# Linear attention feeding two layers on one core: reciprocals on 96x6 through a DMA reshape, the product a step later, and 3.5 slots to a pair of heads

## The chip, the cores and the metric

The kernel runs on one core of a Trainium2 chip. The metric is the device time of one execution in microseconds (us); the kernel before takes 976.46 us, the median of 3 runs (976.12 to 977.76). Engines are named as in the profile: PE (TensorE's matmuls), PEld (its weight loads), DVE (VectorE), ACT (ScalarE), POOL (GpSimd) and SP (SyncE, whose queue issues the DMAs).

## The reference

Three stages in a row, 64-bit weights in, float32 out:

```python
def phi(x):                                   # q, k: (4, 8, 576, 64), w_phi: (64, 128)
    proj = x @ w_phi
    proj = proj - max(abs(proj), axis=-1)
    return concatenate([exp(proj), exp(-proj)])
q_p, k_p = phi(q), phi(k)
kv  = einsum('bhsf,bhsd->bhfd', k_p, v);  z = sum(k_p, axis=2)
num = q_p @ kv;  den = q_p @ z + 1e-06
x = (num / den) as 2304 tokens x 512          # attention's output
x = leaky(x @ w_in) @ w_out                   # first layer, max(0.01 h, h), d_ff 2048
x = silu(x @ w_in2) @ w_out2                  # second layer, h / (1 + exp(-h))
```

## The kernel before

Heads are taken two at a time: 16 pairs. Pairs 0 to 7 are computed in float32 in a prologue (`num_full`). Pairs 8 to 15 are split into a high and a low part (`krh`, `krl`, `qs`, `qh`, `ql`, `KVH`, `KVL`), each product being the sum of three cheaper matmuls, and are computed in the gaps of the first layer (`num_split`, two parts of 288 tokens each).

The first layer has 5 tiles of tokens (`tiles1`) and 16 chunks of 128 hidden features. One chunk of one tile is a slot: there are 80. In a slot `emit_h` runs 12 matmuls (line 528); ACT makes `g` (line 531) and its high part `gh` (401), DVE the rest `gl = g - gh` (`sub`, line 122, the helper behind every `...l` or `...s` tile); `emit_y` of the slot before then runs 12 matmuls on `gh` and `gl` (line 547). In the first 16 slots the weights are also loaded as raw 64-bit numbers, narrowed by DVE (lines 394 to 397: `t`, `r`) and split; later ones come back from DRAM (`load_wo`, line 485, three buffers).

The steps of attention are called at times of a table: `OFF0` for the pairs of the prologue, `OFF1` for the split ones, plus a start `ts` for each pair. Before each half of a slot, `run_att(T0 + STEP * ...)` runs all steps whose time has come; `STEP = W / 4` makes a pair last 4 slots. `missing(t)` makes sure that a tile's tokens are all there before its first slot. A step of pair i, in the order of a pair: `lv`, `lq` load, `sp` splits, `pq0`, `pq1` project q (PE, then an all-reduce of the absolute maximum on POOL, line 223), `pk0`, `pk1`, `pkt` project k (DVE `km` line 152, `ke` line 153, ACT exp), `eq0`, `eq1` make `m`, `qh`, `ql`, `kv` the sums, `num0`, `num1` the quotient. After these calls a scheduler orders the instructions of each engine, so that the order on an engine isn't that of the calls.

In `num_split` the matmuls of line 329 leave in one PSUM bank 64 rows of numerator and 64 rows that all hold the same denominator: ACT copies those to `d` (line 332), DVE takes the reciprocal of 128x288 (line 333) and multiplies each half out of PSUM (line 336), and `put_x` splits the result into the first layer's `xh` and `xl`.

When attention is over, each slot gives 2.0 of credit to `run_jobs`, which prepares the second layer's weights (`prep_wi2`, `prep_wo`, `prep_wo2`, each job at a cost of 1.5 to 3.0). The second layer follows: u = 0 plain, u = 1 and 2 by a scheme of seven products (lines 597, 689, 769).

Of the kernel before, what the change touches and what calls it, by code (L numbers as in the profile page):

```python
# [8 lines left out]
F32 = mybir.dt.float32  # L9
F32R = mybir.dt.float32r  # L10
U32 = mybir.dt.uint32
AF = mybir.ActivationFunctionType
# [7 lines left out]
def tile_linear_attention_ffn_ffn(ctx: ExitStack, tc: tile.TileContext, q, k, v, w_phi, w_in1, w_out1, w_in2, w_out2, out):  # L20


    nc = tc.nc
    B, H, S, D = 4, 8, 576, 64
# [5 lines left out]
    HP = H // 2  # L30
# [3 lines left out]
    RAWB = 2  # L34
    NFULL = 8
    ABUFS0 = dict(kr=3, kt=3, qr=3, va=3, ke=2, p=2, m=2, qh=2, x=2)
    ABUFS1 = dict(kr=2, kt=2, qr=2, va=2, qh=2, ql=2)
    NKV, NNUM = 112, 96
    MIN64, MAX64 = 2.0**-15, 122872.0

# [5 lines left out]
    drp = ctx.enter_context(tc.tile_pool(name="drp", bufs=1, space=DRAM))  # L46
# [5 lines left out]
    def at(shape, dt, tag):  # L52
        return att_pool[0].tile(shape, dt, tag=tag, bufs=AB[0].get(tag, 1), name=tag)
# [28 lines left out]
        nc.vector.tensor_sub(BDL, BDF, BDH.bitcast(F32))  # L82


    tiles1 = [(0, 464)] + [(464 + 460 * i, 460) for i in range(4)]
    X1 = {}

    def x1_tile(t):
# [12 lines left out]
                yield t, lo - a, lo - t0, hi - lo  # L101

    P = [dict() for _ in range(B * HP)]

    def load_qk(i):

        st = P[i]
        st["kr"] = at([128, S0], F32, "kr")
# [15 lines left out]
    def full(i):  # L124
        return i < NFULL
# [102 lines left out]
    def s_eq(a):  # L228
        def f(i):
            st = P[i]  # L230
            c0, n = part(i, a)
            p, m = st["p", a], st["m", a]
            nc.vector.tensor_sub(m, p, m)
            qh = at([128, 2, 2 * n], F32 if full(i) else F32R, "qh")
            st["qh", a] = qh
            if full(i):
                nc.scalar.activation(qh[:, 0], m, AF.Exp)
                nc.scalar.activation(qh[:, 1], m, AF.Exp, scale=-1.0)
                return
# [36 lines left out]
    def put_x(i, rows, src, t0, n):  # L276

        b, hp = i // HP, i % HP
        for t, o, s0, n in segments(b * S + t0, n):
            xh, xl = x1_tile(t)  # L280
            nc.scalar.activation(xh[rows, hp, o : o + n], src[:, s0 : s0 + n], AF.Copy)
            sub(xl[rows, hp, o : o + n], src[:, s0 : s0 + n], xh[rows, hp, o : o + n])
# [34 lines left out]
    def num_split(i, a):  # L317
        st = P[i]
        c0, w = part(i, a)
        d = at([128, w], F32, "d")  # L320
        r = at([128, w], F32, "r")
        x = at([128, w], F32, "x")
        pn = [aps("num"), aps("num")]
        for j in range(2):
            o = pn[j][:, 0:w]
            todo = [(s, g, m) for s in range(2) for g, m in (("KVH", "qh"), ("KVH", "ql"), ("KVL", "qh"))]
            for n, (s, g, m) in enumerate(todo):
                lhs = st[g][:, j, s].rearrange("p t d -> p (t d)")
                nc.tensor.matmul(o, lhs, st[m, a][:, s, j * w : (j + 1) * w], start=(n == 0), stop=(n == 5))  # L329
            den = slice(64, 128) if j == 0 else slice(0, 64)  # L330
            num = slice(0, 64) if j == 0 else slice(64, 128)
            nc.scalar.activation(d[num], o[den], AF.Copy, bias=1e-6)
        nc.vector.reciprocal(r, d)
        for j in range(2):
            num = slice(0, 64) if j == 0 else slice(64, 128)
            nc.vector.tensor_mul(x[num], pn[j][num, 0:w], r[num])
        put_x(i, slice(0, 128), x, c0, w)

    def s_num(a):
        return lambda i: (num_full if full(i) else num_split)(i, a)  # L340

    W, WP = 8.0, 5.0
    fns = dict(
        lq=load_qk, lv=load_v, sp=s_split, pq0=s_pq(0), pq1=s_pq(1),
        pk0=s_pk(0), pk1=s_pk(1), pkt=s_pkt, eq0=s_eq(0), eq1=s_eq(1), kv=s_kv, num0=s_num(0), num1=s_num(1),
    )
    OFF0 = dict(lq=1.1, lv=3.08, sp=3.09, pq0=4.48, pk0=5.33, pk1=5.331, pq1=6.8, eq0=9, pkt=9.13, kv=9.131, num0=11.3, eq1=12.07, num1=16)
    OFF1 = dict(lv=-2.1251, lq=-2.1250, sp=0.5, pq0=2.1172, pk0=4.0606, pk1=4.0616, pq1=4.7479, eq0=6.2094, pkt=7.3391, kv=8.3898, num0=12.1423, eq1=13.9119, num1=14.457)
    END0 = max(OFF0.values()) + 1
    END1 = max(OFF1.values()) + 1  # L350
    ts = [WP * i for i in range(NFULL)]
# [4 lines left out]
    def missing(t):  # L356
        a0, n0 = tiles1[t]
        for _, i, n_ in seq:
            if n_ in ("num0", "num1"):
                c0, w = part(i, int(n_[3]))  # L360
                lo = i // HP * S + c0
                if lo < a0 + n0 and lo + w > a0:
                    return True
        return False

    def run_att(until, tile_=None):
        while seq and (seq[-1][0] < until or (tile_ is not None and missing(tile_))):
            if seq[-1][1] == NFULL and AB[0] is ABUFS0:
                att0_ctx.close()
                att_pool[0] = att_ctx.enter_context(tc.tile_pool(name="att1", bufs=1))  # L370
                AB[0] = ABUFS1
            _, i, n_ = seq.pop()
# [417 lines left out]
    RATE = (9.0, 9.0)  # L790
    s1p = [None]
    PRE = 4
    STEP = W / 4
    T0 = ts[HP - 1] + END0 - 1.15
    make_consts()
    for c in range(PRE):
# [5 lines left out]

    def jobs_of(p):
        for _ in prep_wi2(p):
            yield p, 1.8
        yield p, 1.6
        for f in range(2):
            prep_wo(1, 2 * p + f)
            yield p, 3.0

    def later_jobs():
        for p in range(NC // 2):
            for _ in prep_wo2(p):
                yield NP + p, 1.6
            yield NP + p, 1.5

    jobs = (x for f in (lambda: (x for p in range(NP) for x in jobs_of(p)), later_jobs) for x in f())
    credit, at_p = [0.0], [0]

    def run_jobs(more, upto=-1):  # L820
        credit[0] += more
# [5 lines left out]
    for s, (t, c) in enumerate((t, c) for t in range(len(tiles1)) for c in range(NC)):  # L827
        if t == 0 and c + PRE < NC:
            prep_wi(0, c + PRE)
        wo[c] = prep_wo(0, c) if t == 0 else load_wo(0, c)  # L830
        run_att(T0 + STEP * (s + 0.5) + 0.21, t if c == 0 else None)
        emit_h(t, c)
        run_att(T0 + STEP * (s + 1) + 0.21)
        if prev is not None:
            emit_y(*prev)
        prev = (t, c)
        if not seq and s1p[0] is None:
            att_ctx.close()
# [126 lines left out]
```

## Time and profile before

| | us |
|---|---|
| median of 3 runs | 976.46 (976.12 to 977.76) |
| the profiled execution | 977.25 |
| its span | 975.5 |
| PE busy | 953.0 (98%) |
| DVE busy | 662.0 (68%) |
| ACT busy | 577.1 (59%) |
| POOL busy | 72.6 (7%) |

The span runs from the first to the last instruction; the 1.75 us left of the execution lie around it. An engine is busy while an instruction other than register, branch, semaphore and DMA-issuing ones runs on it. The granted clock is TensorE's, as a share of 2.4 GHz.

### The profile page before, as it was taken

The page shows a single profiled execution, that of the slowest core. Times are in us where ns is not written, and L with a number is a line of the kernel's source. Part 1 is how long each engine was busy: PE and PEld are TensorE (multiplying, and loading weights), DVE is VectorE, ACT ScalarE, POOL GpSimd, SP SyncE. Part 2 cuts the span into 40 slices and gives each one's busy share as a digit, 9 for nine tenths or more (in the row PEclk, how much of TensorE's full clock was granted, in tenths as well). Part 3 has the DMA queues.
Part 4 walks back from the last instruction along what each step waited for, and adds up shares of the span by engine and source line. Part 5 has one row for each costly group of instructions (what it writes and reads, how often), then busy time and mean ns, then how long its engine had stood idle before and what let it go on. Part 6 is the DMA issues. An engine that isn't in the chain of part 4 may idle for free.

```text
span 975.5 us, 15291 instructions
## 1 busy us (share of the span) xinstructions
PE 953.0 (98%) x5328; PEld 879.7 (90%) x5328; DVE 662.0 (68%) x1236; ACT 577.1 (59%) x1171; POOL 72.6 (7%) x38
## 2 busy tenths in 40 slices
PE   7889999989999999999999999999999999999998
PEld 6778888879999999999899999988889999999998
DVE  7998448998666787557667765764557778625853
ACT  6776556676566666555546555664555666544553
POOL 3323200011111111100000000000000000000000
PEclk9999999999999999999999999999999999999999
DMA  8562036874332521218997999998899988897884
GB/s 277 163 207 89 2 131 215 312 240 153 102 96 91 165 86 59 87 52 305 370 322 258 385 412 361 348 374 269 301 357 321 396 271 288 292 296 221 248 275 147
DMA packets 100557, 227.86 MB, mean 234 GB/s; under 512 B 10368, under 2 KB 29568, under 8 KB 100480
## 3 DMA queue, kind: packets, MB, share of 16 engines
q1 hardware_dynamic: 100192, 226.62, 67.3%
q8 instruction: 43, 0.70, 0.3%
q14 instruction: 34, 0.28, 0.1%
q10 hardware_dynamic: 288, 0.26, 0.1%
HBM read 173.36 MB, written 53.48 MB: 233 GB/s over the span
## 4 chain that ended last, share of the span: by engine, by line
PE 83%; DVE 9%; DMA 5%; ACT 2%; issue 1%; SPq 0%; DVEq 0%; ACTq 0%
PE ps_a L528 17%; PE ps_y L547 17%; PE ps_y L769 12%; PE ps_a L597 6%; PE ps_a L689 6%; PE ps_y L689 5%; PE ps_y L630 5%; PE ps_a L262 3%; PE ps_a L329 3%; PE ps_a L630 2%; DMA raw<-in_moe_w_in_dram 2%; DMA raw<-in_moe_w_out_dram 2%; DVE t L396 2%; PE ps_a L296 1%; PE ps_y L262 1%
## 5 line engine op out<-in xcount | busy, mean ns | idle before, releaser
L547 PE MATMUL ps_y<-gh,wo 128*128 128x460 f32 (+1 forms) x640 | 197.0, 372 | 1.6 <-ACT gh L401 1.6
L547 PEld LDWEIGHTS ps_y<-gh,wo 128*128 128x128 f32 x640 | 119.5, 188 | 14.6 <-ACT gh L401 2.4
L547 PE MATMUL ps_y<-gl,wo 128*128 128x460 f32 (+1 forms) x320 | 119.0, 372 | 2.5 <-DVE gl L122 2.4
L528 PE MATMUL ps_a<-xh,wih 128*128 128x460 f32 (+1 forms) x320 | 120.1, 375 | 0.0
L528 PE MATMUL ps_a<-xh,wil 128*128 128x460 f32 (+1 forms) x320 | 118.8, 371 | 0.0
L528 PE MATMUL ps_a<-xl,wih 128*128 128x460 f32 (+1 forms) x320 | 118.7, 371 | 0.0
L769 PE MATMUL ps_y<-gt,ws 128*128 128x384 f32 x672 | 118.2, 337 | 0.0
L769 PEld LDWEIGHTS ps_y<-gt,ws 128*128 128x128 f32 x672 | 117.7, 188 | 0.0
L223 POOL PARTITION_ALL_REDUCE m<-p x32 | 72.0, 2252 | 340.3 <-ACT p L219 199.2
L122 DVE TENSOR_TENSOR gl<-g,gh 128x460 fp32r<-128x460 f32 (+1 forms) x80 | 55.3, 691 | 39.7 <-ACT gh L401 39.0
L531 ACT ACTIVATE g<-ps_a 128x460 f32<-128x460 f32 (+1 forms) x80 | 44.2, 552 | 58.2 <-PE ps_a L528 55.5
L689 PE MATMUL ps_a<-xs,ws 128*128 128x384 f32 x378 | 71.8, 336 | 0.6 <-DVE g L668 0.5
L547 PEld LDWEIGHTS ps_y<-gl,wo 128*128 128x128 f32 x320 | 60.1, 188 | 9.6 <-DVE gl L122 3.4
L689 PEld LDWEIGHTS ps_a<-xs,ws 128*128 128x128 f32 x378 | 66.0, 188 | 1.6 <-DVE g L668 0.8
L528 PEld LDWEIGHTS ps_a<-xh,wil 128*128 128x128 f32 x320 | 60.2, 188 | 6.7
L528 PEld LDWEIGHTS ps_a<-xh,wih 128*128 128x128 f32 x320 | 60.2, 188 | 6.3 <-issue 0.3
L597 PE MATMUL ps_a<-xs,ws 128*128 128x384 f32 x336 | 65.7, 338 | 0.0
L528 PEld LDWEIGHTS ps_a<-xl,wih 128*128 128x128 f32 x320 | 60.2, 188 | 6.1
L597 PEld LDWEIGHTS ps_a<-xs,ws 128*128 128x128 f32 x336 | 60.0, 188 | 3.1 <-DVE hs L589 0.3
L392 ACT ACTIVATE t<-raw 128x512 f32<-128x512 f32 x64 | 42.7, 668 | 32.1 <-DMA raw<-in_moe_w_out_dram 16.2
L401 ACT ACTIVATE gt<-g 128x384 fp32r<-128x384 f32 x80 | 41.8, 524 | 33.6 <-PE ps_y L769 33.1
L122 DVE TENSOR_TENSOR gt<-g,gt 128x384 fp32r<-128x384 f32 x80 | 44.2, 555 | 23.8 <-ACT gt L401 23.5
(168 smaller groups left out, 1852.7 us busy)
## 6 DMA issues: line engine op xcount, KB each, us to landing
ws<-wis SPq DMA_DIRECT2D x168, 256.0 KB, 5.2
wo<-wos SPq DMA_DIRECT2D x80, 512.0 KB, 5.1
raw<-in_moe_w_in_dram SPq DMA_DIRECT2D x32, 512.0 KB, 5.0
raw<-in_moe_w_out_dram SPq DMA_DIRECT2D x32, 512.0 KB, 5.4
wos<-wo SPq DMA_DIRECT2D x32, 512.0 KB, 5.1
ws<-wo SPq DMA_DIRECT2D x64, 256.0 KB, 4.1
wis<-wst SPq DMA_DIRECT2D x24, 512.0 KB, 6.4
ws<-wos SPq DMA_DIRECT2D x48, 256.0 KB, 3.9
```

The source lines that it names most:

```text
L122: nc.vector.tensor_tensor(out_, x, h.bitcast(F32), op=ALU.subtract)
L223: nc.gpsimd.partition_all_reduce(m, p, 128, bass_isa.ReduceOp.absmax)
L262: nc.tensor.matmul(pv[:, s, j], ke[:, 2 * c + j, s, :], vf[:, w : w + NKV], start=False, stop=(j == 1 and c == 3), skip_group_check=True)
L392: nc.scalar.activation(t, hi.bitcast(F32), AF.Abs)
L401: nc.scalar.activation(h, f, AF.Copy)
L528: nc.tensor.matmul(ph, a[:, kk, :], b_[:, kk, :], start=(m == 0), stop=(m == 3 * KD - 1))
L531: nc.scalar.activation(g, ph, AF.Prelu, alpha=0.01)
L547: nc.tensor.matmul(Y[t][d][:, 0:n], a[:, ds_], b_, start=(c == 0 and m == 0), stop=(c == NC - 1 and m == 2))
L597: nc.tensor.matmul(bank[b_], w[:, a, kk], x[:, c, kk], start=(first and m == 0), stop=(m == 5), skip_group_check=True)
L630: nc.tensor.matmul(Y[u][r], a[:, rs], hl[f][:, b_], start=(p == 0 and f == 0 and m == 0), stop=(p == NC // 2 - 1 and f == 1 and m == 2))
L689: nc.tensor.matmul(bank[b_], w[:, a, kk], x[:, c, kk], start=(first and m == 0), stop=(m == 5), skip_group_check=True)
L769: nc.tensor.matmul(bank[b_][db], w[:, a, db], t[:, c], start=(first and p == 0 and m == 0), stop=(p == NP - 1 and m == 2), skip_group_chec ...
```

## The change

Six edits, made together.

- In `num_split` ACT copies one row of denominators (1x288) for each half and the numerators (64x288) to `x`. The two rows go by DMA into `e6` (96x6), DVE takes the reciprocal there, a DMA writes it to `rec` in DRAM, and two DMAs broadcast it back over 64 partitions each into `d`.
- The product of `x` and `d` and `put_x` move to new steps `fin0`, `fin1`, at 16 and 18.3 in `OFF1`; `missing` looks for these.
- `x` and `d` get two buffers each.
- `pkt` moves from 7.3391 to 5.1 in `OFF1`.
- `STEP` is `W / 3.5`, so a pair lasts 3.5 slots; `tiles1` is 462, 462, 460, 460, 460 in place of 464 and four of 460.
- `settle` ends a half-done job of weight preparation before the next part of the second layer's `x` is prepared.

```diff
-    ABUFS1 = dict(kr=2, kt=2, qr=2, va=2, qh=2, ql=2)
+    ABUFS1 = dict(kr=2, kt=2, qr=2, va=2, qh=2, ql=2, x=2, d=2)
...
-    tiles1 = [(0, 464)] + [(464 + 460 * i, 460) for i in range(4)]
+    tiles1 = [(462 * i, 462) for i in range(2)] + [(924 + 460 * i, 460) for i in range(3)]
...
+    rec = drp.tile([B * HP, 2, S], F32, name="rec")
...
         d = at([128, w], F32, "d")
-        r = at([128, w], F32, "r")
-        x = at([128, w], F32, "x")
+        x = st["x", a] = at([128, w], F32, "x")
...
-            den = slice(64, 128) if j == 0 else slice(0, 64)
+            den = slice(64, 65) if j == 0 else slice(0, 1)
             num = slice(0, 64) if j == 0 else slice(64, 128)
-            nc.scalar.activation(d[num], o[den], AF.Copy, bias=1e-6)
-        nc.vector.reciprocal(r, d)
+            nc.scalar.activation(d[den], o[den], AF.Copy, bias=1e-6)
+            nc.scalar.activation(x[num], o[num], AF.Copy)
+
+        e = at([96, w // 48], F32, "e6")
         for j in range(2):
-            num = slice(0, 64) if j == 0 else slice(64, 128)
-            nc.vector.tensor_mul(x[num], pn[j][num, 0:w], r[num])
-        put_x(i, slice(0, 128), x, c0, w)
+            nc.sync.dma_start(e[48 * j : 48 * j + 48], d[64 - 64 * j : 65 - 64 * j])
+        nc.vector.reciprocal(e, e)
+        nc.sync.dma_start(rec[i, a].rearrange("(p f) -> p f", p=96), e)
+        st["r", a] = d
+        for j in range(2):
+            nc.sync.dma_start(d[64 * j : 64 * j + 64], rec[i, a, j * w : (j + 1) * w].unsqueeze(0).to_broadcast([64, w]))
+
+    def s_fin(a):
+        def f(i):
...
+            nc.vector.tensor_mul(x, x, st["r", a])
+            put_x(i, slice(0, 128), x, c0, w)
...
-    OFF1 = dict(lv=-2.1251, lq=-2.1250, sp=0.5, pq0=2.1172, pk0=4.0606, pk1=4.0616, pq1=4.7479, eq0=6.2094, pkt=7.3391, kv=8.3898, num0=12.1423, eq1=13.9119, num1=14.457)
+    FIN = 16
...
+    OFF1 = dict(lv=-2.1251, lq=-2.1250, sp=0.5, pq0=2.1172, pk0=4.0606, pk1=4.0616, pq1=4.7479, eq0=6.2094, pkt=5.1, kv=8.3898, num0=12.1423, eq1=13.9119, num1=14.457, fin0=FIN, fin1=FIN + 2.3)
...
-            if n_ in ("num0", "num1"):
+            if n_ in ("fin0", "fin1"):
...
-    STEP = W / 4
+    STEP = W / 3.5
...
+    def settle():
+
+        while half[0]:
+            credit[0] -= next(jobs)[1]
```

Since the steps fall into other slots, the scheduler gives each engine another order. Three places show it.

The first is DVE's order from the `gl` of slot 10 to that of slot 12, in the stretch where the last weights are narrowed (`t`, `r`, `wo`). Before:

```order
L122 TENSOR_TENSOR gl<-g,gh 128x464
L122 TENSOR_TENSOR qs<-qr,qs 64x576 x2
L122 TENSOR_TENSOR wo_1808<-r_1810,wo_1808 128x512
L122 TENSOR_TENSOR gl<-g,gh 128x464
L394 TENSOR_SCALAR t_1866<-t_1866 128x512
L395 TENSOR_SCALAR t_1866<-t_1866 128x512
L396 SCALAR_TENSOR_TENSOR t_1866<-raw,t_1866 128x512
L122 TENSOR_TENSOR gl<-g,gh 128x464
```

Now, the last twelve of the rows up to slot 12's `gl` (slot 11's stands eight rows above the first):

```order
L413 TENSOR_SCALAR t_1901<-t_1901 128x512
L123 TENSOR_TENSOR kth<-kt,kth 64x128
L412 TENSOR_SCALAR t_1983<-t_1983 128x512
L153 TENSOR_REDUCE km<-ps_a 128x1
L414 SCALAR_TENSOR_TENSOR t_1901<-raw,t_1901 128x512
L413 TENSOR_SCALAR t_1983<-t_1983 128x512
L123 TENSOR_TENSOR ql<-e,qh 128x576
L154 TENSOR_TENSOR ke<-ps_a,km 128x128
L415 ISA r_1902<-t_1901,r_1902 128x1024
L414 SCALAR_TENSOR_TENSOR t_1983<-raw,t_1983 128x512
L123 TENSOR_TENSOR ql<-m,qh 128x576
L123 TENSOR_TENSOR gl<-g,gh 128x462
```

Steps of the first split pairs (`kth`, `km`, `ke`, `ql`) have moved in among the narrowing, and nineteen rows stand between the two `gl` in place of three.

The second is DVE's order in the steady part, around one part's quotient. Before:

```order
L333 RECIPROCAL r<-d 128x288
L122 TENSOR_TENSOR ql<-e,qh 128x576
L122 TENSOR_TENSOR ql<-m,qh 128x576
L336 TENSOR_TENSOR x<-ps_a,r 64x288 x2
L122 TENSOR_TENSOR qs<-qr,qs 64x576 x2
L122 TENSOR_TENSOR xl<-x,xh 128x232
L122 TENSOR_TENSOR xl<-x,xh 128x56
L122 TENSOR_TENSOR gl<-g,gh 128x460
```

Now (line 338 is the reciprocal on 96x6, line 351 the product of `fin0` or `fin1`):

```order
L351 TENSOR_TENSOR x<-x,d 128x288
L234 TENSOR_TENSOR m<-p,m 128x576
L123 TENSOR_TENSOR gl<-g,gh 128x462
L123 TENSOR_TENSOR xl<-x,xh 128x232
L123 TENSOR_TENSOR xl<-x,xh 128x56
L338 RECIPROCAL e_2606<-e_2606 96x6
L123 TENSOR_TENSOR ql<-e,qh 128x576
L123 TENSOR_TENSOR ql<-m,qh 128x576
L123 TENSOR_TENSOR gl<-g,gh 128x462
L351 TENSOR_TENSOR x<-x,d 128x288
L123 TENSOR_TENSOR KVL<-ps_a,KVH 128x2x64
L123 TENSOR_TENSOR xl<-x,xh 128x288
```

The reciprocal and the product of a part are apart now, and a `gl` follows each of them within a few rows.

The third is SP's queue in the steady part. Before:

```order
L111 DMA kr<-in_k_dram 128x512
L485 DMA wo_2699<-wos 128x1024
L485 DMA wo_2781<-wos 128x1024
L113 DMA qr<-in_q_dram 128x576
L112 DMA kt<-in_k_dram 128x128
L485 DMA wo_2825<-wos 128x1024
```

Now:

```order
L337 DMA e_2796<-d 48x1x6
L112 DMA kr<-in_k_dram 128x512
L337 DMA e_2796<-d 48x1x6
L503 DMA wo_2941<-wos 128x1024
L339 DMA rec<-e_2796 96x6
L342 DMA d<-rec 64x288 x2
L114 DMA qr<-in_q_dram 128x576
```

The five transfers of a part stand among the loads, here with a `wo` load (line 503 now) between `e6` and `rec`.

## Rows read from the trace of the kernel before

**Rows 1.** The page's first part: busy us, share of the span, instructions.

```profile
PE 953.0 (98%) x5328; PEld 879.7 (90%) x5328; DVE 662.0 (68%) x1236; ACT 577.1 (59%) x1171; POOL 72.6 (7%) x38
```

**Rows 2.** Busy time by stage: PE, PEld, DVE, ACT, POOL, clock, DMA share, GB/s.

```profile
0.00:118.00 118.00, 103.55 (x741) 87.09 (x741) 94.11 (x199) 83.16 (x183) 37.73 (x22) 0.99 0.46 153
...
167.60:218.00 50.40, 46.31 (x240) 40.44 (x239) 46.63 (x86) 37.41 (x73) 4.94 (x2) 0.97 0.78 264
218.00:650.00 432.00, 432.00 (x2336) 396.93 (x2335) 294.65 (x511) 256.03 (x510) 29.98 (x14) 1.00 0.63 221
650.00:850.00 200.00, 199.35 (x1066) 188.68 (x1065) 130.34 (x260) 113.12 (x237) 0.00 (x0) 1.00 0.90 314
```

**Rows 3.** PE's timeline from 167 to 218.5 us: start, duration, instruction, wait and releaser.

```profile
167.61 0.46 PE L547 MATMUL ps_y<-gh,wo 128*128 128x464 f32 x1
...
203.92 1.11 PE L547 MATMUL ps_y<-gh,wo 128*128 128x464 f32 x4 [0.96 <-ACT gh L401]
207.41 0.47 PE L547 MATMUL ps_y<-gl,wo 128*128 128x464 f32 x1 [2.39 <-DVE gl L122]
...
217.71 0.29 PE L216 MATMUL ps_a<-qs,BDL 128*128 128x288 f32 x1
217.84 0.37 PE L547 MATMUL ps_y<-gh,wo 128*128 128x464 f32 x1
218.06 0.37 PE L547 MATMUL ps_y<-gl,wo 128*128 128x464 f32 x1
```

**Rows 4.** Busy time in the stretch at half clock, columns as in rows 2.

```profile
208.70:212.10 3.40, 3.40 (x16) 3.22 (x15) 3.37 (x8) 2.33 (x5) 0.00 (x0) 0.50 0.87 254
```

**Rows 5.** DVE's waits from 164.6 to 208.85 us: total, times, longest.

```profile
DVE t L394 <- ACT t L392: 2.7, 3, 1.7
```

**Rows 6.** DVE's timeline from 167 to 209 us, columns as in rows 3.

```profile
168.12 0.43 DVE L394 TENSOR_SCALAR t<-t 128x512 f32<-128x512 f32 x1 [1.71 <-ACT t L392]
...
188.44 1.52 DVE L394 TENSOR_SCALAR t<-t 128x512 f32<-128x512 f32 x1
189.99 0.99 DVE L395 TENSOR_SCALAR t<-t 128x512 uint32<-128x512 uint32 x1
...
203.78 0.69 DVE L396 SCALAR_TENSOR_TENSOR t<-raw,t 128x512 uint32<-128x512 uint32 x1
204.38 1.78 DVE L122 TENSOR_TENSOR wo<-r,wo 128x512 fp32r<-128x512 f32 x1
```

**Rows 7.** POOL's timeline from 185 to 260 us.

```profile
188.27 2.43 POOL L223 PARTITION_ALL_REDUCE m<-p  x1 [71.69 <-DMA qr<-in_q_dram]
203.95 2.51 POOL L223 PARTITION_ALL_REDUCE m<-p  x1 [13.25 <-DVE ql L122]
```

**Rows 8.** DVE's busy time between the ends of two `gl`, with its instructions.

```profile
164.60:208.85 44.25, 40.82 (x75) 1.00 0.75 255
```

**Rows 9.** DVE's instructions by form: count, busy us, mean ns, idle before.

```profile
L333 DVE RECIPROCAL r<-d 128x288 f32<-128x288 f32 x16 | 31.2, 1949 | 2.0 <-ACT d L332 2.0
...
L336 DVE TENSOR_TENSOR x<-ps_a,r 64x288 f32<-64x288 f32 x32 | 14.5, 452 | 0.5
...
L122 DVE TENSOR_TENSOR xl<-x,xh 128x288 fp32r<-128x288 f32 x8 | 3.7, 459 | 5.0 <-ACT xh L281 5.0
...
L306 DVE RECIPROCAL d<-d 128x6 f32<-128x6 f32 x8 | 1.5, 182 | 0.1
```

**Rows 10.** ACT's copies of the denominators, columns as in rows 9.

```profile
L332 ACT ACTIVATE d<-ps_a 64x288 f32<-64x288 f32 x32 | 13.0, 406 | 3.3 <-PE ps_a L329 2.3
```

**Rows 11.** The `kt` loads (64 KB) from 118 to 340 us.

```profile
DMA to landing us min/median/max: 1.8/2.9/5.8
```

**Rows 12.** DMA issues from 212 to 450 us: count, KB each, median us to landing.

```profile
wo<-wos SPq DMA_DIRECT2D x33, 512.0 KB, 3.3
```

**Rows 13.** SP's waits from 212 to 450 us: total, times, longest.

```profile
SPq L485 <- PE ps_y L547: 91.6, 22, 14.6
```

**Rows 14.** PE's waits from 650 to 850 us.

```profile
PE ps_a L689 <- DVE g L668: 0.5, 1, 0.5
```

More of the change, by code (lines that the diff above doesn't have):

```diff
@@ L329, in num_split @@
                 nc.tensor.matmul(o, lhs, st[m, a][:, s, j * w : (j + 1) * w], start=(n == 0), stop=(n == 5))
-            den = slice(64, 128) if j == 0 else slice(0, 64)
+            den = slice(64, 65) if j == 0 else slice(0, 1)
             num = slice(0, 64) if j == 0 else slice(64, 128)
-            nc.scalar.activation(d[num], o[den], AF.Copy, bias=1e-6)
-        nc.vector.reciprocal(r, d)
+            nc.scalar.activation(d[den], o[den], AF.Copy, bias=1e-6)
+            nc.scalar.activation(x[num], o[num], AF.Copy)
+        e = at([96, w // 48], F32, "e6")
         for j in range(2):
-            num = slice(0, 64) if j == 0 else slice(64, 128)
-            nc.vector.tensor_mul(x[num], pn[j][num, 0:w], r[num])
-        put_x(i, slice(0, 128), x, c0, w)
+            nc.sync.dma_start(e[48 * j : 48 * j + 48], d[64 - 64 * j : 65 - 64 * j])
[6 more added lines that the diff above has]
+        def f(i):
+            if full(i):
+                return
+            st = P[i]
+            c0, w = part(i, a)
+            x = st["x", a]
+            nc.vector.tensor_mul(x, x, st["r", a])
+            put_x(i, slice(0, 128), x, c0, w)
+        return f
     def s_num(a):
@@ L344, in tile_linear_attention_ffn_ffn @@
         lq=load_qk, lv=load_v, sp=s_split, pq0=s_pq(0), pq1=s_pq(1),
-        pk0=s_pk(0), pk1=s_pk(1), pkt=s_pkt, eq0=s_eq(0), eq1=s_eq(1), kv=s_kv, num0=s_num(0), num1=s_num(1),
+        pk0=s_pk(0), pk1=s_pk(1), pkt=s_pkt, eq0=s_eq(0), eq1=s_eq(1), kv=s_kv, num0=s_num(0), num1=s_num(1), fin0=s_fin(0), fin1=s_fin(1),
     )
-    OFF0 = dict(lq=1.1, lv=3.08, sp=3.09, pq0=4.48, pk0=5.33, pk1=5.331, pq1=6.8, eq0=9, pkt=9.13, kv=9.131, num0=11.3, eq1=12.07, num1=16)
-    OFF1 = dict(lv=-2.1251, lq=-2.1250, sp=0.5, pq0=2.1172, pk0=4.0606, pk1=4.0616, pq1=4.7479, eq0=6.2094, pkt=7.3391, kv=8.3898, num0=12.1423, eq1=13.9119, num1=14.457)
+    FIN = 16
+    OFF0 = dict(lq=1.1, lv=3.08, sp=3.09, pq0=4.48, pk0=5.33, pk1=5.331, pq1=6.8, eq0=9, pkt=9.13, kv=9.131, num0=11.3, eq1=12.07, num1=16, fin0=11.3001, fin1=16.0001)
+    OFF1 = dict(lv=-2.1251, lq=-2.1250, sp=0.5, pq0=2.1172, pk0=4.0606, pk1=4.0616, pq1=4.7479, eq0=6.2094, pkt=5.1, kv=8.3898, num0=12.1423, eq1=13.9119, num1=14.457, fin0=FIN, fin1=FIN + 2.3)
     END0 = max(OFF0.values()) + 1
@@ L804, in jobs_of @@
         for _ in prep_wi2(p):
+            half[0] = True
             yield p, 1.8
+        half[0] = False
         yield p, 1.6
@@ L813, in later_jobs @@
             for _ in prep_wo2(p):
+                half[0] = True
                 yield NP + p, 1.6
+            half[0] = False
             yield NP + p, 1.5
     jobs = (x for f in (lambda: (x for p in range(NP) for x in jobs_of(p)), later_jobs) for x in f())
-    credit, at_p = [0.0], [0]
+    credit, at_p, half = [0.0], [0], [False]
+    def settle():
+        while half[0]:
+            credit[0] -= next(jobs)[1]
     def run_jobs(more, upto=-1):
@@ L843, in tile_linear_attention_ffn_ffn @@
                 if c in (3, 6):
+                    settle()
                     next(x_first)
@@ L870, in tile_linear_attention_ffn_ffn @@
         if p in (4, 6):
+            settle()
             next(nxt, None)
```

## The prediction

> **What bounds the kernel now.** I read the page's engine line first: PE is busy for 953.0 of 975.5 us, DVE 68%, ACT 59% [rows 1]. So the time is PE's matmuls plus the places where PE has nothing to do, and the next question is where those are. The table by stage [rows 2] answers: from 218 to 650 us PE is busy without a gap, with DVE at 294.65 of 432 us. An edit that only relieves DVE there buys nothing. PE idles in the prologue (14.5 us up to 118), in the stretch from 167.6 to 218 us (4.1), and a little from 650 to 850 (0.65).
>
> The diff leaves the prologue's eight pairs alone, and up to the `gl` of slot 8 (a slot is one chunk of the first layer for one tile) the work is the same, so the prologue's 14.5 us stay. Open to the change are the stretch after slot 8, the steady part in which the split pairs run, and 650 to 850.
>
> In the stretch PE's timeline names the releasers: 0.96 us for `gh` (ACT) at 203.92, 2.39 for `gl` (DVE) at 207.41 [rows 3]. Right after them PE runs from 208.70 to 212.10 at a granted clock of 0.50, its 1.2 GHz level [rows 4]; at full clock that work takes half as long, so 1.7 us are lost. The second products of slot 8 start at 167.61 and those of slot 15 at 217.84, 50.23 us apart. Matmuls follow one another at full clock every 0.21 us (460 columns) and 0.13 us (288) [rows 3]; 168 of the first kind make 35.1 us and the attention's, counted in the order at such steps, 8.0, so 43.1 in all. 7.1 us are stall: 4.1 idle, 1.7 of clock, the rest restarts with longer steps.
>
> Why was `gl` late at 207? DVE waits 2.7 us for the raw weights [rows 5], and three of its 512-wide instructions are stretched while GpSimd runs an all-reduce of 2.43 or 2.51 us [rows 7]: 1.52 and 0.99 where such a row takes 0.43, 1.78 where it takes 0.69 [rows 6]. That is 2.7 us for two all-reduces, 1.4 each. Between the ends of the `gl` of slots 8 and 15, 164.60 and 208.85, DVE works 40.82 of 44.25 us [rows 8]. DVE and PE are about level here; it is the only stretch in which a DVE instruction costs time.
>
> **The change part by part.**
>
> *The reciprocal.* A part (half a pair's tokens) loses a reciprocal of 128x288, 1.949 us, and two products of 0.452; it gains a reciprocal on 96x6 and one product of 128x288, which the trace lacks. Nearest are the 128x6 reciprocal, 0.182, and the 128x288 `xl`, 0.459 [rows 9]. DVE saves 2.85 - 0.64 = 2.2 us a part, 35 over 16 parts. I count 0 of it: they all stand after 218 us, where PE has no gap [rows 2]. Uncovered it would be the whole 35. ACT makes four copies a part for two. A copy from one partition is bounded by 0 and by the 0.406 of 64 partitions [rows 10]; I take 0.41, as its row is as long. That is 0.8 us a part, 13 in all, on an engine with 256 of 432 us busy there [rows 2]: nothing.
>
> *The DMAs.* Each part sends five small transfers through SP: two of `d` to `e6`, one of `e6` to DRAM, two back as a broadcast; 80 in all, none of the kind in the trace. Nearest is the 64 KB `kt` load, 1.8 us at best and 5.8 at worst beside the raw loads [rows 11]. Copy, link, reciprocal, link, link make 0.41 + 1.8 + 0.18 + 1.8 + 1.8 = 6.0 us up to the product. It reaches the path where DVE comes to the reciprocal or the product before its data, with a `gl` behind it: the second excerpt shows such places. Walked along DVE's rows by their durations, no `gl` is late there while a link takes up to about 2.5 us. Where a `wo` load stands on SP between `e6` and `rec` (some half of the parts, third excerpt) `rec` waits for it too, and these loads wait for PE, 4.2 us on average (91.6 over 22) [rows 13]. I take 0.2 us for each of 3.5 groups of two pairs, **+0.7**; bounds 0 (links of 1.8) and 1.5 each, +5.
>
> *Moved past.* SP's waiting `e6` and `rec` also hold back `wo`, `kr`, `kt`, `qr` behind them. A `wo` load lands in 3.3 us, and 33 of them, one a slot, go out in 238 us [rows 12]: 7.2 us a slot, 3.9 of cover. 0.
>
> *3.5 slots to a pair.* Pairs follow closer and the first starts a slot or two earlier. In the steady part PE's work is the same, dealt out differently: 0. But the first pairs now meet the last narrowing of weights, in the stretch above. By the orders, between the `gl` of slots 8 and 15 DVE goes from 73 instructions to 106: among the 33 are eight more of k features, four of `ql`, two of `m`, two of `qs`, four `KVL`, eight of narrowing, four `s` sums. Without what the all-reduces took, the old ones average (40.82 - 2.7) / 75 = 0.51 us [rows 8]; that makes 16.8. PE gains less there: 12 matmuls of 0.21, 28 of 0.13, 12 of 256 and 2 of 128 columns, 7.7 us by their starts, to 50.8. There are four all-reduces with their `m` or data in it for two.
>
> DVE then needs 40.8 + 16.8 + 2 x 1.4 = 60.4 us from 164.60, plus 0 to 2.7 of waiting for raw weights: slot 15's `gl` ends at 225.0 to 227.7. PE unstalled would want it at 167.61 + 50.8 = 218.4. It is late by 6.6 to 9.3 us, for 7.1 before. I take 7.9, **+0.8**. Bounds: -1.4 (less waiting for weights than any row shows, cheaper all-reduces) and +5.1 (all-reduces that stop DVE for their 2.47 us).
>
> The first excerpt shows where: before, seven rows covered two `gl`; now nineteen rows lie between the `gl` of slots 11 and 12. I expect PE's longest wait there, some 4.9 us.
>
> *The later part.* Of PE's 0.65 us idle from 650 to 850 [rows 2], 0.5 waits for DVE's `g` [rows 14] beside rows that prepare the second layer's weights; about 1 us more goes in slower starts. That preparation is paid by 2.0 of credit a slot once attention is over, and four more slots follow then, so it ends before this stretch. **-0.8**; bounds -1.6 (all gone) and +0.5. `settle` finishes half-done jobs ahead of an x preparation, under the same full PE: 0. `tiles1` keeps 2304 columns: 0.
>
> **Sum.** 0.8 + 0.7 - 0.8 = +0.7 us. The profiled run took 977.25, its span 975.5 and 1.75 around it; it lies 0.8 above the median of 976.46. So 977.95 for such a run, **977.2** as a median.
>
> **A rule to weigh.** Beside the all-reduce that began at 203.95 and ended at 206.46, the `wo` row with two SBUF inputs took 1.78 for 0.69 and ended at 206.16, before the all-reduce [rows 6, 7]. The Trainium skill's "SBUF — State Buffer", section "Who interferes with whom", says that a VectorE instruction with two SBUF inputs contends with a GpSimd instruction that reads SBUF, and that the second to issue is fully blocked until the first is done. The row bears out the contention and not the full block; by the rule four all-reduces would cost 9.9 us where the rows make 5.6, and the sum would be +5.0. It speaks against this change besides, since the new product of `x` by `d` has both inputs in SBUF where the old ones read one from PSUM.
>
> **The rivals.**
>
> *VectorE stands still for the whole all-reduce (slower).* For: the rows at 188.44 and 189.99 lie almost wholly under one, and the earlier pairs put four of them into the stretch for two. Each costs 2.47 for 1.4, +4.3: **981.5**. It decides from about 1.9 us an all-reduce. Against: at 204.38 the loss was 1.1 of 2.51 [rows 6, 7].
>
> *The DMA chain holds VectorE (slower).* A link over 2.5 us, or `rec` behind a `wo` load that waits for PE, and the product makes the next `gl` late by 1 to 1.5 us in each of 3.5 groups: **980 to 981.7**. For: SP is one queue, and its longest `wo` wait is 14.6 us [rows 13]. Against: the transfers are small, and `kt` lands in 1.8 when little else moves [rows 11].
>
> *The stretch gets better (faster).* The pair's work fills DVE's 2.7 us of waits for raw weights and the run at 1.2 GHz does not come: -1.4 - 1.7, and the later stalls go, -0.8: with +0.7 about **973**. Against: 33 more rows on the engine that was late.
>
> *The change does nothing to the bound (the forecast).* The 35 us saved lie under a full PE, and the terms of either sign stay near 1 us.
>
> **How the numbers follow.** 0.2% (2 us) is about what a measurement of this kernel can tell from no change. Chances: forecast, within 2 us, 0.40; VectorE stopped 0.20; DMA chain 0.15; stretch better 0.25. The bounds of all terms add up to -3 and +10.6, which need everything at once; the range 973.3 to 982 leaves out the ends of the outer cases, some 2 in 10. The forecast's own range is 975.2 to 979.
>
> **What would show it.** Right: PE without gaps from about 230 to 650 us; DVE some 30 us less busy from 250 to 450; PE's longest wait of the stretch on the `gl` of slot 12; no wait for `g` near 755. Wrong: PE waits for `gl` behind a product of `x` by `d` after 230 us (the chain); DVE rows of 2 us and more beside all-reduces (the block); no wait at slot 12 (the stretch better).

## The result, and the profile after

The changed kernel takes 986.17 us (median of 4 runs, 984.71 to 988.14) where the kernel before took 977.11 beside it (976.12 to 978.31): the ratio is 1.0095, interval 1.0074 to 1.0117. It is 9 us slower; 977.2 was forecast as the likeliest and 982.0 as the upper end. The profiled execution took 984.99, its span 983.1, 7.6 more than the span of before.

The page's first part, and below it the table by stage with the columns and windows of [rows 2]:

```profile
PE 956.0 (97%) x5328; PEld 878.9 (89%) x5328; DVE 625.1 (64%) x1220; ACT 585.4 (60%) x1203; POOL 76.9 (8%) x38
```

```profile
0.00:118.00 118.00, 103.80 (x742) 87.54 (x743) 94.08 (x200) 83.24 (x183) 37.52 (x22) 0.99 0.45 153
167.60:218.00 50.40, 46.04 (x252) 40.15 (x251) 48.50 (x88) 40.21 (x80) 11.10 (x3) 1.00 0.77 268
218.00:650.00 432.00, 426.65 (x2277) 387.53 (x2276) 260.15 (x502) 261.04 (x533) 28.29 (x13) 1.00 0.66 230
650.00:850.00 200.00, 200.00 (x1067) 189.38 (x1066) 118.65 (x235) 107.45 (x224) 0.00 (x0) 1.00 0.86 293
```

VectorE is relieved as forecast, 662 to 625 us in all. But the part from 218 to 650 us, where PE had no gap, now has 5.35 us of them; the prologue is as it was, and from 650 to 850 nothing is left of the 0.65.

Windows cut the program at different places in the two runs, so I set the stalls against the program instead: for each matmul the distance to the next start, less the median distance of matmuls of that form in the trace of before, summed between the starts of second products of the same slots.

| stall us, up to slot | 8 | 8 to 20 | 20 to 42 | 42 to 79 | 79 to the end | sum |
|---|---|---|---|---|---|---|
| before | 19.1 | 7.3 | 0.4 | -0.3 | 3.3 | 29.7 |
| changed | 19.0 | 10.0 | 3.1 | 3.0 | 2.2 | 37.2 |

The sums differ by 7.5 us, which is what the traces differ by from the first matmul to the last (967.6 and 975.1). Three stretches lose, 2.8, 2.7 and 3.2 us, and the end gains 1.1. Two limits of this table. Each row is one execution, and single executions of one kernel lie some us apart. And the 7.3 of before hold the 1.7 us that its run at 1.2 GHz costs [rows 4]; the changed kernel's trace has no such run behind slot 8 (granted clock 1.00 in both windows above). Without it slots 8 to 20 lose 4.4 us rather than 2.8.

What VectorE waits for in the steady part is new. Its longest waits from 212 to 430 us (total, times, longest):

```profile
DVE x L351 <- DMA d<-rec: 43.9, 16, 5.9
DVE gl L123 <- ACT gh L419: 13.4, 11, 3.9
```

Every one of the sixteen products stops VectorE, 2.7 us on average. Few of these stops reach PE: three do so with 0.5 us or more, 2.0 us at 236, 1.0 at 283 and 0.5 at 268. Take the first of them across the engines. First SP's timeline, the transfers of one part:

```profile
222.58 0.59 SPq L337 DMA_DIRECT2D e<-d  x1
...
223.98 0.53 SPq L337 DMA_DIRECT2D e<-d  x1
...
226.20 0.33 SPq L503 DMA_DIRECT2D wo<-wos  x1
226.72 0.32 SPq L339 DMA_DIRECT2D rec<-e  x1
227.14 1.05 SPq L573 DMA_DIRECT2D x<-o  x2
232.34 1.13 SPq L342 DMA_DIRECT2D d<-rec  x2
```

Then VectorE's, ScalarE's and PE's timelines at the same place:

```profile
231.15 0.29 DVE L123 TENSOR_TENSOR KVL<-ps_a,KVH 128x128 fp32r<-128x128 f32 x1 [0.34 <-ACT KVH L274]
235.87 0.46 DVE L351 TENSOR_TENSOR x<-x,d 128x288 f32<-128x288 f32 x1 [4.42 <-DMA d<-rec]
```

```profile
236.36 0.44 ACT L282 ACTIVATE xh<-x 128x288 fp32r<-128x288 f32 x1 [4.60 <-DVE x L351]
236.71 0.26 ACT L274 ACTIVATE KVH<-ps_a 128x128 fp32r<-128x128 f32 x1
236.86 0.55 ACT L549 ACTIVATE g<-ps_a 128x462 f32<-128x462 f32 x1
```

```profile
237.46 0.48 PE L546 MATMUL ps_a<-xh,wih 128*128 128x462 f32 x1 [1.71 <-ACT g L549]
```

The reader is to see a wait handed on. The write of `rec` is issued at 226.72, and SP issues the broadcast at 232.34, when the write has landed. The product waits 4.42 us; ScalarE stands 4.60 us before `xh`, and behind it in ScalarE's order is the `g` of a slot, which has to empty a PSUM bank before PE can go on. The stop at 283 is plainer: the product waits, a `gl` stands behind it, and PE waits for that `gl`. From VectorE's and PE's timelines:

```profile
282.20 0.46 DVE L351 TENSOR_TENSOR x<-x,d 128x288 f32<-128x288 f32 x1 [1.67 <-DMA d<-rec]
282.58 0.63 DVE L123 TENSOR_TENSOR gl<-g,gh 128x462 fp32r<-128x462 f32 x1
```

```profile
283.27 0.47 PE L565 MATMUL ps_y<-gl,wo 128*128 128x462 f32 x1 [0.84 <-DVE gl L123]
```

From the second `e6` at 223.98 to the product at 235.87 are 11.9 us, for 5.6 in my sum; over the sixteen parts it is 6.7 to 11.9, 8.9 in the median. By links, least, median and most from issue to landing are:

```profile
L337 SPq DMA_DIRECT2D e<-d x32: 533/539/646, 211.4 to 416.3; - x32
...
DMA to landing us min/median/max: 1.7/1.7/3.9
```

```profile
L339 SPq DMA_DIRECT2D rec<-e x16: 319/326/351, 219.8 to 419.1; - x16
...
DMA to landing us min/median/max: 1.4/2.2/5.6
```

```profile
L342 SPq DMA_DIRECT2D d<-rec x32: 482/546/596, 221.4 to 421.9; - x32
...
DMA to landing us min/median/max: 2.5/2.9/5.4
```

The third loss lies behind the end of attention and the last product. Its largest piece is 1.0 us; the others are 0.5 or less. ScalarE's timeline there:

```profile
430.60 0.54 ACT L549 ACTIVATE g<-ps_a 128x460 f32<-128x460 f32 x1
435.96 0.63 ACT L419 ACTIVATE wst<-s 128x512 fp32r<-128x512 f32 x1 [4.82 <-DMA wis<-wst]
436.50 0.57 ACT L419 ACTIVATE gh<-g 128x460 fp32r<-128x460 f32 x1
```

and SP's:

```profile
426.55 1.28 SPq L503 DMA_DIRECT2D wo<-wos  x3
427.87 0.43 SPq L447 DMA_DIRECT2D wis<-wst  x1
428.34 0.66 SPq L503 DMA_DIRECT2D wo<-wos  x1
430.03 9.86 SPq L447 DMA_DIRECT2D wis<-wst  x3
```

Four `wo` loads go out together around the first store of prepared weights; the buffer of `wst` comes free 8 us after that store, and a slot's `gh` stands behind `wst`. PE's next matmul, on `gh`, starts 1.04 us late; the profile names no releaser for it, but that `gh` ends at 437.07:

```profile
437.17 1.06 PE L565 MATMUL ps_y<-gh,wo 128*128 128x460 f32 x4 [0.87 <-issue]
```

### The profile page after: what moved, and what is told of

It is laid out like the page before. It is cut to its first block, busy times and chain, and to the rows that moved or that the text cites. A ratio compares the mean times of both kernels' runs of the same rounds, so it can differ in the third digit from the quotient of the medians.

```text
span 983.1 us, 15487 instructions
## 1 busy us (share of the span) xinstructions
PE 956.0 (97%) x5328; PEld 878.9 (89%) x5328; DVE 625.1 (64%) x1220; ACT 585.4 (60%) x1203; POOL 76.9 (8%) x38
## 4 chain that ended last, share of the span: by engine, by line
PE 73%; DMA 10%; DVE 10%; ACT 4%; issue 2%; SPq 0%; DVEq 0%; ACTq 0%
PE ps_y L565 13%; PE ps_a L546 13%; PE ps_y L787 12%; PE ps_a L707 7%; PE ps_a L615 6%; PE ps_y L707 5%; PE ps_y L648 5%; PE ps_a L648 2%; DMA raw<-in_moe_w_in_dram 2%; DMA raw<-in_moe_w_out_dram 2%; PE ps_a L329 2%; PE ps_y L263 2%; PE ps_a L263 2%; DVE t L414 2%; DMA d<-rec 2%
## 5 line engine op out<-in xcount | busy, mean ns | idle before, releaser
L565 PE MATMUL ps_y<-gh,wo 128*128 128x460 f32 (+1 forms) x640 | 199.6, 373 | 3.7 <-ACT wo L419 1.8
L224 POOL PARTITION_ALL_REDUCE m<-p x32 | 76.3, 2386 | 314.1 <-ACT p L220 96.2
```

What stands on the lines that cost most here:

```text
L224: nc.gpsimd.partition_all_reduce(m, p, 128, bass_isa.ReduceOp.absmax)
L565: nc.tensor.matmul(Y[t][d][:, 0:n], a[:, ds_], b_, start=(c == 0 and m == 0), stop=(c == NC - 1 and m == 2))
```

## The experiments

Theory A was that VectorE's stops at the product, behind the chain of transfers, make most of the loss; the rivals were B, the pace (3.5 slots crowd the engines), and C, the small transfers holding up weight loads in SP's order. Each kernel was timed in 5 rounds against the kernel before on its chip.

**e1: the old pace.**

```diff
-    STEP = W / 3.5
+    STEP = W / 4
```

> The changed kernel with 4 slots to a pair again; the DMA chain, the late product, pkt, tiles and settle stay. Times are given beside 977 before and 986 after. Theory A (VectorE stops at the product until the broadcast has come back; 5.6 us of the 7.5 us that the traces differ by): the chain is as long, but each pair has half a slot more, so most of the stops stay, 980 to 983, with VectorE still waiting 30 us or more at the product. Theory B (the pace: 3.5 slots crowd the engines and let the weight preparation start early): back to 977, the stall between slots 15 and 36 under 1 us. Theory C (the small transfers hold up the weight loads on SP): 982 to 986, PE waiting for wo or wih.

980.02 us beside 976.63, ratio 1.0023 (1.0006 to 1.0039). VectorE still waits at all sixteen products, 49.1 us from 200 to 470 us, and yet the loss is a quarter. So a stop at the product is cheap at four slots to a pair. The time is the low end of A's figures and the wait within them; but three quarters of the loss go when the pace does, which was B's point. Its traced execution took 983.20, the slowest of its twelve, with one run at 1.2 GHz in slots 8 to 20.

**e2: the new pace alone.** The kernel before with `STEP = W / 3.5`, and `settle` so that it can run:

```diff
-    STEP = W / 4
+    STEP = W / 3.5
...
+                    settle()
                     next(x_first)
```

> The kernel before with 3.5 slots to a pair, and with settle, without which the x preparation can find the raw buffers taken; reciprocals on VectorE as before, no new DMAs. A: no stop at a product, so only the weight preparation that starts earlier costs, some 2 to 3 us: 978 to 980. B: 984 to 986, like the changed kernel, or more, since VectorE carries its 35 us of reciprocals at the faster pace. C: 977 to 980, as A.

997.93 us, ratio 1.0219 (1.0195 to 1.0243): far above A, and above B's figure too, which said "or more". Its trace has PE gaps all over the steady part: 221.7 of 232 us busy.

```profile
218.00:450.00 232.00, 221.70 (x1275) 201.63 (x1274) 160.51 (x260) 141.62 (x294) 28.75 (x13) 0.99 0.32 111
```

VectorE works 160.51 us there, so it is not full. The old quotient reads PSUM twice more after a reciprocal of 1.95 us, so its two banks are held that long. That this is what 3.5 slots can't bear is inferred: PE's longest waits there are for `gl` (4.2 us), `g` and `o`, and e3 differs from e2 in the copy out of PSUM, the later product and the small edits together.

**e3: no transfers.** The changed kernel with VectorE's own reciprocal, still in place before the later product:

```diff
-        e = at([96, w // 48], F32, "e6")
...
-        nc.vector.reciprocal(e, e)
...
+        nc.vector.reciprocal(d, d)
+        st["r", a] = d
```

> The changed kernel with the reciprocal of 128x288 on VectorE again and none of the five transfers; the product still stands in fin0 and fin1 on SBUF inputs, ACT still copies numerators, 3.5 slots. A: the stops at the product go, VectorE gets 31 us of reciprocals back under a full PE: 979 to 981, the stall from slot 15 to 36 under 2 us. B: 986 or more. C: 979 to 981 too, so e4 has to tell A from C.

982.06 us, ratio 1.0051 (1.0033 to 1.0068): 4 us of the 9 come back though VectorE does its 31 us of reciprocals again. So A holds for about that much, and not for all; the time lies between the two forecasts. By the traces, the stall of slots 8 to 20 stays, at 10.2 us; slots 20 to 42 go from 3.1 to 1.4, and slots 42 to 79, behind the last product, from 3.0 to -0.2.

**e4: transfers, but no wait.**

```diff
-            nc.vector.tensor_mul(x, x, st["r", a])
+            nc.vector.tensor_mul(x, x, x)
```

> The changed kernel with the product taken of x and x instead of x and d: all five transfers still run on SP, but nothing waits for the broadcast. It leaves out the division, so the values differ. A: 979 to 981, like e3, the stall from slot 15 to 36 under 2 us. B: 985 to 987. C: 984 to 987, since the transfers are still in SP's queue.

982.87 us, ratio 1.0057 (1.0039 to 1.0074), like e3. All eighty transfers are in SP's queue and only the wait is gone, and e3, which has none of them, is only 0.8 better: so C is out as the main cause. By its figure the time decides nothing, 1.9 us above A's range and 1.1 below C's. The stall of slots 20 to 42 falls from 3.1 to 1.1. Of slots 42 to 79 2.2 us stay, where e3 has none.

**e5: weight preparation from slot 46 as before.**

```diff
         if s1p[0] is not None:
-            run_jobs(2.0)
+            if s >= 46:
+                run_jobs(2.0)
```

> The changed kernel, but the credit for weight preparation starts at slot 46 as before, though attention ends four slots earlier. Theory A (the weight preparation that starts early costs the 3.2 us of stalls that the traces show from slot 42 to 79): these go and the 1.1 us gained after 640 us come back, 2 us less than the changed kernel, 984. Theory B (those stalls come from how full VectorE and ScalarE are in general, wherever the jobs stand): they move along, 986.

986.21 us, ratio 1.0087 (1.0065 to 1.0109): B by the time, which is that of the changed kernel. The trace doesn't settle it: 1.4 us of the stalls of slots 42 to 79 are left in it, but that execution took 981.16 us at a granted clock of 1.00, 5 us less than the median of its six. By the median, when the jobs start is not what costs.

**e6: `rec` and the broadcasts on POOL's queue.**

```diff
-        nc.sync.dma_start(rec[i, a].rearrange("(p f) -> p f", p=96), e)
+        nc.gpsimd.dma_start(rec[i, a].rearrange("(p f) -> p f", p=96), e)
```

(the same for the two broadcasts).

> The changed kernel with the write of rec and the two broadcasts issued by POOL in place of SP; e6 stays on SP. Theory A (the chain is long because its links stand in SP's order behind weight loads and stores, and the links themselves take 2 us): VectorE's wait at the product falls from 44 us to under 25 and the kernel gains 2 to 3 us, 983 to 984. Theory B (the three links themselves, 1.7 and 2.2 and 2.9 us in the median, make the chain): the wait stays above 35 us and the time within 2 us of 986, or worse where POOL's all-reduces wait behind them.

983.37 us, ratio 1.0058 (1.0046 to 1.0070). VectorE's wait at the product from 212 to 430 us:

```profile
DVE x L351 <- DMA d<-rec: 24.8, 10, 4.2
```

As A had it, wait and time. But A's reason is not borne out: the chain did not get shorter. The landings in this kernel, of `e6`, `rec` and the broadcasts:

```profile
DMA to landing us min/median/max: 1.7/1.7/4.2
DMA to landing us min/median/max: 1.6/2.4/5.1
DMA to landing us min/median/max: 2.5/2.9/4.3
```

From the issue of the second `e6` to the last landing the sixteen parts take 9.5 us in the median, for 8.8 in the changed kernel. The wait fell because VectorE's order is another: six products stand far enough back that their data had landed. Nor does the gain lie where the products are. From slot 15 to 42 the stall is 5.5 us, for 5.8 in the changed kernel: the stop at 236 is gone, and others of 0.8 to 1.5 us have come at 294, 351 and 390. The gain is behind the last product, -0.3 in place of 3.0 in slots 42 to 79.

**e7: attention 2.5 slots later.** `run_att(T0 + STEP * (s + 0.5 - 2.5) + 0.21, ...)`, and likewise in the second call.

> The changed kernel with the attention of the first layer started 2.5 slots later, still at 3.5 slots to a pair; VectorE has 81 instructions between the gl of slots 8 and 15 in place of 106, before has 73. Theory A (of the 9 us about 1 to 3 lie in the crowd of slots 8 to 16, about 5 in the stops at the product, 3 in the weight preparation): 1 to 3 less by the crowd, and up to 2 by the preparation that starts later, 981 to 984, with VectorE's wait at the product still above 35 us. Theory B (the pace alone): no change, 986.

983.20 us, ratio 1.0067 (1.0054 to 1.0080), as A, with VectorE waiting 37.8 us at the product. The stall of slots 8 to 20 is 7.8 us for 10.0, though it holds a run at 1.2 GHz (1.7 us) that the changed kernel's doesn't. Slots 42 to 79 stay at 2.8.

**e8: e3, 2.5 slots later.**

> The kernel of e3 (reciprocal of 128x288 on VectorE, no transfers, product in the later step, 3.5 slots) with the attention started 2.5 slots later. Theory A: neither stops at the product nor the crowd, 976 to 979, that is the time of before within what can be measured. Theory B (the pace): 982, as e3.

980.13 us, ratio 1.0024 (1.0009 to 1.0038): 2.6 us better than e3, and still 2 above before. A by direction, missed by 1 us.

**e9: e3 at the old pace.** The product in a later step and the small edits, nothing else.

> The kernel of e3 at 4 slots to a pair: beside before it has only the product in a later step with ACT's copies of the numerators, pkt, tiles1 and settle. Theory A (the chain and the pace are all that costs; the small edits and the late product cost nothing under a full PE): 976 to 978, like before, and the 2.2 us that e1 lost belong to the chain. Theory B (the later product and the small edits cost by themselves): 979 to 980, like e1.

976.55 us, ratio 1.0013 (1.0000 to 1.0026). A: these edits cost at most 2.5 us, and perhaps nothing. PE's stall of slots 8 to 20 is 5.1 us; the 7.3 of before are 5.6 without the run at half clock of [rows 4], which this trace doesn't have (granted clock 1.00 there).

**e10: e6 and e7 together.**

> The changed kernel with rec and the broadcasts on POOL's queue (as e6, 2.8 us less) and attention 2.5 slots later (as e7, 3 us less). If the two costs are apart, as Theory A has it, the gains add: 980 to 981. If both took away the same stops (Theory B), 983.

986.06 us, ratio 1.0102 (1.0086 to 1.0119): neither. The gains don't add, they vanish. In its trace the stalls are 9.4 us in slots 8 to 20, 5.0 up to 42 and 3.6 up to 79. Three runs at 1.2 GHz account for a good part of them, two in the first stretch and one in the last (columns as in [rows 2]):

```profile
180.10:183.50 3.40, 3.40 (x11) 2.97 (x10) 2.77 (x7) 2.89 (x7) 0.00 (x0) 0.50 0.95 338
210.80:214.20 3.40, 3.40 (x19) 3.40 (x18) 3.37 (x6) 0.00 (x0) 2.33 (x1) 0.50 0.78 311
466.80:470.20 3.40, 3.40 (x11) 2.94 (x10) 3.37 (x7) 1.97 (x5) 0.00 (x0) 0.50 1.02 395
```

Each costs 1.7 us, 5.1 in all, and each comes just behind a stop of PE, of 1.7, 2.5 and 1.9 us; the changed kernel's trace has none behind slot 8. Over the whole program the four executions of e10 were granted 0.993 to 0.995, the four of the changed kernel 0.996 to 0.998. Taking each execution's time at lost clock out (an estimate from these figures: its span times what the clock lacks of 1) leaves e10 2.5 us below the changed kernel, near Theory B's 3. By this estimate the two gains overlap, and the clock takes the rest away. What brings its falls stays open.

**e11: e3, 4.5 slots later.**

> The kernel of e3 with attention 4.5 slots later, still 3.5 slots to a pair; VectorE has 64 instructions between the gl of slots 8 and 15, fewer than before (73). Theory A (PE's stall in slots 8 to 16 follows VectorE's work there): that stall falls from 7.2 to under 5 us, 974 to 977, at or below before. Theory B (the stall comes from raw weights and ScalarE's share, whatever stands on VectorE): 979 to 981, as e8.

978.19 us, ratio 1.0022 (1.0008 to 1.0036): neither quite. Up to slot 15 the stall is 4.8 us as A had it, and 2.9 more come between slots 15 and 20, where the pair's work now stands: 7.7 in all. Of the first 4.8, 1.7 are a run at 1.2 GHz behind a stop of 2.0 us.

**e12: POOL's queue at the old pace.**

> The changed kernel at 4 slots to a pair with rec and the broadcasts on POOL's queue. Theory A (the chain costs through VectorE's stops at the product, shorter on POOL's queue, and through the small transfers in SP's order at the end of attention): 976 to 978, the 2 to 3 us of e1 gone. Theory B (the links themselves): 980, as e1.

979.13 us, ratio 1.0034 (1.0019 to 1.0049): no gain over e1, though VectorE's wait at the product falls from 49.1 to 18.5 us (200 to 470 us). At four slots a shorter wait buys nothing that shows. Rather B.

No version beat the kernel before.

## Why the prediction was wrong, point by point

Four kernels make a square: with and without the transfers, at 4 and at 3.5 slots to a pair. By the ratios, in us over the 977 of before:

| | 4 slots | 3.5 slots |
|---|---|---|
| reciprocal on VectorE, product later (e9, e3) | +1.3 (0 to 2.5) | +5.0 (3.2 to 6.6) |
| through DMAs (e1, changed) | +2.2 (0.6 to 3.8) | +9.3 (7.2 to 11.4) |

The pace costs 3.7 us without transfers and 7.1 with them; the transfers 0.9 at the old pace and 4.3 at the new. The 3.4 us by which the two together exceed their sum are no larger than the intervals allow, so that they feed each other is not shown. With each execution's time at lost clock taken out as for e10 (an estimate; before by its runs beside e1 to e12), the transfers cost 2.6 and about 3.5, hardly more at the new pace, and the pace 6.7 and about 7.5.

*The reciprocal, 35 us saved and counted as 0: right.* e3 has them back and is 4 us faster than the changed kernel; where they stand, in slots 20 to 42, it stalls for 1.4 us.

*The DMAs, +0.7 with bounds 0 and 5: the step that failed first.* Having the transfers cost 4.3 us at this pace, 0.7 inside the upper bound and six times what was taken. The mechanism was named, as the second rival, and the size was off. I priced each link with the best landing of a `kt` load, 1.8 us, where [rows 11] have 2.9 in the median and 5.8 at worst; the links' medians were 1.7, 2.2 and 2.9, with 5.6 at worst, and the whole chain took 8.9 us for 5.6. And I had "no `gl` is late while a link takes up to about 2.5 us" from a walk along VectorE's rows alone. At 283 a `gl` was late behind the product, as the rival had it; the larger stop, at 236, went through ScalarE: `xh` behind the product, a slot's `g` behind `xh`. The three stops seen on PE behind products make 3.5 us of the trace. That they are the whole of the 4.3 is not shown: e6 cuts VectorE's wait by four tenths and gains 0.3 us where the products stand, and e3 and e6 gain 3 us behind the last product.

*Moved past, 0: wrong in part.* PE never waits for a weight load there, so the cover that I worked out held; the largest piece of the loss came by the stores of prepared weights. At 3.5 slots the kernels with the transfers on SP stall from slot 42 to 79 (changed 3.0 us, e4 2.2, e5 1.4, e7 2.8), those without them don't (e3 -0.2, e8 -0.4, e11 -0.3). At four slots the gap is smaller (e1 1.7, e9, without transfers, 0.9). e6 (-0.3) and e10 (3.6), with two of the three links on POOL, differ, so it is the order at that place and not the transfers as such; what sets it was not found.

*3.5 slots to a pair, +0.8 against before: near in its own window by luck, and the window was too short.* I priced slots 8 to 15 at 7.9 us for 7.1. The traces have 7.3 in them before and 7.4 now. But 1.7 of the 7.3 are the run at half clock, which did not come now, as the third rival had it; without it PE's stalls there grew by 1.8. They were not one wait of 4.9 for the `gl` of slot 12 either: the longest stands at slot 12, but with 1.4 us and for `wo` (ScalarE), and half a dozen others, of 0.4 to 1.3, are for `wo`, `qs`, `gl`, `p` and `g`. What I left out comes right behind slot 15, 2.7 us up to slot 20. The stop at 236, the chain's, is 2.0 of them; yet e3, without any transfer, has 2.1 there too, 1.7 of it behind a late `gl`.

The sum of instructions, 73 to 106, was right, and what it costs goes with it, roughly:

| | e9 | before | e11 | e7 | e8 | e10 | changed | e3 | e4 |
|---|---|---|---|---|---|---|---|---|---|
| VectorE instructions between `gl` 8 and 15 | 77 | 73 | 64 | 81 | 81 | 81 | 106 | 106 | 109 |
| stall of slots 8 to 20, us | 5.1 | 7.3 | 7.7 | 7.8 | 8.7 | 9.4 | 10.0 | 10.2 | 11.1 |
| of it lost at 1.2 GHz | 0 | 1.7 | 1.7 | 1.7 | 1.7 | 3.4 | 0 | 0 | 0 |

Without the clock's share the kernels with 64 to 81 instructions stall for 5.1 to 7.0 us and those with 106 to 109 for 10.0 to 11.1. Inside either group the stall doesn't follow the number. So at 3.5 slots without a shift these stretches lose 4 to 5 us (changed against before 4.4, e3 against e9 5.1), and the late product by itself changes them by no more than 0.5 (e9 against before), by these single traces.

*The later part, -0.8: right*, -1.1 in the trace.

*Small edits and product later, 0: right* within 0.3% (e9).

*VectorE stopped for the whole all-reduce, the first rival: not seen.* The all-reduce at the crowded place was itself held up. POOL's timeline of the changed kernel:

```profile
195.87 5.66 POOL L224 PARTITION_ALL_REDUCE m<-p  x1 [13.12 <-DVE ql L123]
```

and VectorE's beside it:

```profile
196.84 0.69 DVE L123 TENSOR_TENSOR wo<-r,wo 128x512 fp32r<-128x512 f32 x1
197.44 0.64 DVE L123 TENSOR_TENSOR gl<-g,gh 128x462 fp32r<-128x462 f32 x1
...
198.32 0.69 DVE L123 TENSOR_TENSOR wo<-r,wo 128x512 fp32r<-128x512 f32 x1
```

These rows of two SBUF inputs take what they take elsewhere, and the all-reduce 5.66 us for 2.5 [rows 7]. Later in the same all-reduce, and beside the next, VectorE's rows are the ones that are stretched, by 0.6 and 1.1 us:

```profile
199.73 1.06 DVE L412 TENSOR_SCALAR t<-t 128x512 f32<-128x512 f32 x1 [0.37 <-ACT t L410]
209.33 1.52 DVE L412 TENSOR_SCALAR t<-t 128x512 f32<-128x512 f32 x1
```

No row of VectorE beside an all-reduce takes 2 us behind slot 8; the longest is 1.84. So four all-reduces in the stretch took 3.8 us from VectorE, for 5.6 in my sum.

Of the signs named, two came: VectorE 33 us less busy from 250 to 450 us (139.1 to 105.7), and no wait for `g` near 755. PE without gaps from 230 did not, and PE's wait for a `gl` behind a product, the sign of the chain, did. Of the 7.5 us that the traces differ by, then, none lies in the window that I had priced, 5.4 lie in slots 15 to 42, where the pairs run at the new pace with the chain, and 3.2 behind them; 1.1 come back at the end.

## What to carry to other kernels

A stop on an engine with time to spare can be paid by what stands behind it in the orders of the others, as at 236: after a new wait, follow the waiting instruction's readers through each in-order engine until a PE input or a PSUM bank is reached, not only along its own engine. Price a chain of small DMAs by the median of loads in the same stretch and by the issue order, and ask what is left to cover its length when the pace rises too (the chain cost 0.9 us at four slots to a pair and 4.3 at three and a half, a difference within the intervals). A smaller total of waits on one engine is no gain by itself: in e6 and e12 the wait fell by 40% and more, and PE's stalls where the products stand hardly fell with it in e6, nor the time in e12. Follow a loss past the end of the stretch that was priced. Before stalls of two traces are compared, take out what each lost at the lower clock. And when two edits are made together, run the square of them.

## What the runs showed of the hardware

- Three dependent small DMAs (2 x 1.1 KB in SBUF, 2.3 KB to DRAM, two broadcasts back over 64 partitions) take 6.7 to 11.9 us from the issue of the second `e6` transfer to use, 8.9 in the median: 313.07 to 319.76 at best, 223.98 to 235.87 beside stores and a 512 KB load. In the median SP issues `rec` 0.3 us after the landing of `e6`, the reciprocal lying between, and the broadcast 0.02 after that of `rec`; so the links themselves make most of it.
- ScalarE's copy of 288 elements takes 0.39 us from one partition where 64 partitions took 0.41 [rows 10].
- Beside a dense run of VectorE one all-reduce of GpSimd took 5.66 us, where the others behind slot 8 took 2.1 to 2.9, also in the traces of e3, e5 and e6, while VectorE's rows kept their 0.64 to 0.69; beside the others a row of VectorE is stretched, by up to 1.1 us. So these traces have either engine losing. The profile's spans on GpSimd are rough.
- TensorE's runs at 1.2 GHz behind slot 8 last 3.4 us, cost 1.7 each, and come just behind stops of PE of 1.7 to 2.9 us (before, e1, e2, e7, e8, e10, e11); stops of 2.3 us (e7, at 211) and 1.7 (the changed kernel, at 237) had none behind them. How many there are differs between executions: 27 of the kernel before were granted 0.993 to 1.000 and took 979.2 to 972.5 us.
